# Two chained MLPs on one core: where the block-product weights of the second are built

## The chip, the cores and the metric

One NeuronCore of a Trainium2 chip runs the whole program. The metric is the device time of one execution in microseconds (us), as the median of several. Five engines work side by side, each through its own queue in order: PE (matmuls), ACT, DVE and POOL (elementwise work), and SP, which here issues all DMAs. Products are in float32, kept exact enough by splitting each operand into a rounded high half and a low half (operand minus high half) and adding three matmuls.

## The reference

Attention with packed keys gives x of 4608 tokens by 512. Two MLPs follow:

```python
a = x @ w_a;  b = x @ w_b                 # 512 -> 1536
y = (a * b) @ w_out                       # 1536 -> 512
h = y @ w_in                              # 512 -> 2048
g = h * clip(h + 3, 0, 6) / 6
out = g @ w_out2                          # 2048 -> 512
```

## The kernel before

The first MLP runs in four groups of 1152 tokens, each in twelve steps (`t`, with `m` = 0 to 11 inside a group) over the hidden width. In a step PE runs four `ab_unit` and one `pw_unit`; `y_unit`s follow three steps later and fill in between. Beside that, a list `bg` of small background units (Python functions that each emit a few instructions) is spread over the steps: in each step `nb` of them, `nb` being what is left of the list divided by the steps left before the last one, rounded up, and these over the step's ten slots. In the first three groups `bg` holds attention; in the last group (`g + 1 == NG`, 628 to 787 us in the profile) it holds the preparation of the second MLP: the y operands of the first tile of tokens (`y_units`) and the weights of the first block (`w_prep`). The last `y_unit`s run alone up to 806 us.

The second MLP runs over six tiles of 768 tokens (`tt`), each in eight blocks (`p`) of 256 hidden columns. A block computes its 2 x 2 block product h by the Strassen-Winograd scheme: seven products (`prod`, 6 matmuls of 384 columns each) in the order 1, 6, 2, 7, 5, 4, 3, into three PSUM banks' worth of results x, y and z that share two banks. DVE adds partial results (u2, u3, c22, c21, c12, all at L744), ACT and DVE apply the gate (`gate`, L751 and L753), and `parts` splits the gated block into g2h and g2l (L759, L760). Twelve output units (`o_unit`, three matmuls of 512 columns each) of the block before stand between the products: two after product 1, two after product 2, two after product 5, six after product 3. The first block of the first tile has none. In the profile the results are named h_px, h_py, h_pz for block p.

A product needs a weight operand out of `w` (128 x 3584 numbers per block: seven block matrices, high and low). Three of the seven are the raw blocks a11, a12, a22, four are sums of raw blocks. `w_prep` builds them once, in the first tile: `load` (L496) fetches two raw pieces, `wo_load` (L526) two raw pieces of the output weights, `sums` (L504 to L508) makes s1 to s4 on POOL, `parts` (L517, L518) copies to the high half on ACT and subtracts on POOL, `store` (L522) writes w to DRAM (`w2d`), and `wo_parts` (L533, L534) splits the output weights. The build of block p + 1 is put into the list `side` during block p. From the second tile on, `w_load` (L487) fetches the finished w, one block ahead. w has one buffer in each of two pools, used in turn. The raw weights, the raw output weights and the raw y data of the next tile (`y_load`, L546) all use one buffer, tag `raw`, in the pool `p2a`.

`side` is emptied in program order at fixed places of a block: `some(3)` after product 1 and two output units, `some(2)` after product 2, `some(2)` after product 5, `some(2)` and `some(9)` at the end. In block 6 of a tile the y load of the next tile and its three first differences on POOL (`y_first`) join the list. In block 7 `swap(k)` makes the next tile's operand for product k right after product k has run: a copy on ACT (L566) and a subtraction on DVE or POOL (L567).

Of the kernel before, what the change touches and what calls it, by code (L numbers as in the profile page):

```python
# [8 lines left out]
F32 = mybir.dt.float32  # L9
F32R = mybir.dt.float32r  # L10
# [11 lines left out]
DM, F1, F2 = 512, 1536, 2048  # L22
P = 128
# [7 lines left out]
NW = NM2 // 2  # L31
QK_SCALE = 1.0 / 8.0
CP = 512
# [7 lines left out]
def f32(ap):  # L41
    return ap.bitcast(F32)
# [3 lines left out]
def tile_kernel(ctx: ExitStack, tc: tile.TileContext, qT, kT, vn, pT, wab, wo1, win, wo2, out):  # L46
# [9 lines left out]
    act, dve, pool, pe, sp = nc.scalar, nc.vector, nc.gpsimd, nc.tensor, nc.sync  # L56
# [46 lines left out]
    p2f = dram.tile([NM2, 2, P, CP], F32, name="p2f")  # L103
# [378 lines left out]
    def w_tile(pool_, p, tt):  # L482
        w_t[p] = pool_.tile([P, 2, 7, 2, P], F32R, tag="w", name=f"w{tt}_{p}")
        return w_t[p]

    def w_load(pool_, p, tt):
        sp.dma_start(f32(w_tile(pool_, p, tt).rearrange("p h a k n -> p (h a k n)")), w2d[p])  # L487

    def w_prep(rpool, pool_, p):

        z = {}

        def load():
            z["r"] = rpool.tile([P, 6, CP], F32, tag="raw", name=f"raw_w{p}")
            for i in range(2):
                sp.dma_start(z["r"][:, i], p2f[2 * p + i, 0])  # L496

        def sums(lo):
            def fn():
                x = z["r"].rearrange("p i (k n) -> p i k n", k=2)  # L500
                a11, a12, a21, a22 = x[:, 0, 0], x[:, 0, 1], x[:, 1, 0], x[:, 1, 1]
                s1, s2, s3, s4 = x[:, 2, 0], x[:, 2, 1], x[:, 3, 0], x[:, 3, 1]
                if lo:
                    pool.tensor_sub(s3, a11, a21)  # L504
                    pool.tensor_sub(s4, a12, s2)
                else:
                    pool.tensor_add(s1, a21, a22)
                    pool.tensor_sub(s2, s1, a11)  # L508
            return fn

        def parts(of, a, n):
            def fn():
                if "w" not in z:
                    z["w"] = w_tile(pool_, p, 0).rearrange("p h a k n -> p h (a k n)")
                x = z["r"].rearrange("p i n -> p (i n)")[:, of * 256:(of + n) * 256]
                hi, lo = (z["w"][:, i, a * 256:(a + n) * 256] for i in range(2))
                act.copy(hi, x)  # L517
                pool.tensor_sub(lo, x, f32(hi))  # L518
            return fn

        def store():
            sp.dma_start(w2d[p], f32(z["w"].rearrange("p h x -> p (h x)")))  # L522

        def wo_load():
            for i in range(2):
                sp.dma_start(z["r"][:, 4 + i], p2f[2 * p + i, 1])  # L526

        def wo_parts(opool, i):
            def fn():
                hi = opool.tile([P, DM], F32R, tag=f"wo2_hi{p}{i}", name=f"wo2_hi{2 * p + i}")  # L530
                lo = opool.tile([P, DM], F32R, tag=f"wo2_lo{p}{i}", name=f"wo2_lo{2 * p + i}")
                wo2_t[2 * p + i] = (hi, lo)
                act.copy(hi, z["r"][:, 4 + i])  # L533
                pool.tensor_sub(lo, z["r"][:, 4 + i], f32(hi))  # L534
            return fn

        return [load, wo_load, sums(0), sums(1), parts(0, 0, 2), parts(3, 2, 1), parts(4, 3, 4), store], lambda o: [wo_parts(o, 0), wo_parts(o, 1)]

    def y_units(pool_, tt):

# [106 lines left out]
    p2a = None  # L647
# [16 lines left out]
    for t in range(NSTEP):  # L664
        g, m = divmod(t, NM1)
        if m == 0 and g + 1 < NG:
            lhs_tiles(g + 1)
            bg = att_units(2 * g + 2) + att_units(2 * g + 3)
        if m == 0 and g + 1 == NG:
            sp.dma_start(*stores[-1])  # L670
            es_att.close()
            p2a = es_p2a.enter_context(tc.tile_pool(name="p2a", bufs=1, side="right", reuse_waits="tile"))
            y_load, y_first, y_part = y_units(p2a, 0)
            prep, wo_prep = w_prep(p2a, p2a, 0)
            bg = [y_load, lambda: None, lambda: None] + y_first + [y_part[k] for k in (1, 6, 2, 7, 5, 4, 3)] + prep
# [12 lines left out]
        if t == 0:  # L688
            n_conv = 4
        elif g == 0:  # L690
            n_conv = sum(x < NM1 for x in (m + 2, m + 1, m + 3))
        else:
            n_conv = 2 * NM2 * (t - NM1 + 1) // (2 * NM1) - 2 * NM2 * (t - NM1) // (2 * NM1) if g < 3 else 0
        parts = spread(list(range(5 * n_conv)), 9 if n_conv > 2 else 6) + [[]] * 4
        now = []
        for i, (u, *x) in enumerate(units):
            if (u.__name__[:2], *x) not in ahead:
                u(*x)
            tick()
            if i == 1:  # L700
                wab_load(t + 3)
            if m % SW < 2 and i in ((3, 4) if t == 0 else (1, 2)):
                wo_split(t, i - (3 if t == 0 else 1))
            if m % SW == 1 and i in (3, 4):
                wo_split(t + 1, i - 3)
            if i in (3, 4) and m == NM1 - 1 and g + 1 < NG:
                at_split(2 * g + 3, (i - 3,))
            for k in range(2):
                for _ in parts[2 * i + k]:
                    if not now:  # L710
                        now = piece_units()
# [13 lines left out]
    with (  # L725
# [29 lines left out]
        def parts(i, j):  # L755
            n = 1 if i == j else 2
            hi, lo = tmp(f"g2h{i}{j}", n, F32R), tmp(f"g2l{i}{j}", n, F32R)
            u = u_t.pop((i, j))
            act.copy(hi, u)  # L759
            dve.tensor_sub(lo, u, f32(hi))  # L760
            g_t2[i, j] = (hi, lo)
# [32 lines left out]
                if side:  # L794
                    side.pop(0)()

        side.extend(wo_prep(p2b))
        for tt in range(NTT):
            for p in range(NW):
                now[:] = [tt, p]  # L800
                more = tt + 1 < NTT
                nxt = (p + 1) % NW
                wpool = (p2a, p2b)[nxt % 2]
                if tt == 0 and p + 1 < NW:
                    prep, wo_prep = w_prep(p2a, wpool, p + 1)
# [106 lines left out]
```

## Time and profile before

| | us |
|---|---|
| median of 3 runs (1589.46 to 1590.21) | 1590.19 |
| the profiled execution's own time | 1588.73 |
| its span, first to last instruction | 1587.0 |
| PE busy in the span | 1499.7 (95%) |
| DVE, ACT, POOL busy | 874.9, 682.0, 528.8 |

The rows below come from several views. The table of stretches gives, for each stretch, the busy time of each engine in it (x the number of its instructions), the granted clock of PE as a share of full speed, the busy share of the DMA engines and what they moved. A timeline lists instructions in order of time: start, duration, engine, line, operation, output <- inputs, and in brackets how long the engine sat idle before it and what ended that. A group row gives busy time and mean duration of equal instructions. A wait row says who waited for whom, the total, how often and the longest. A row of DMA issues gives the number, the size of each and the median time from issue to landing.

### The profile page before, as it was taken

Reading aid. Unit: us, or ns where it says so; the run is one execution under the profiler, and the core shown is the slowest. Engines: PE = TensorE matmul, PEld = TensorE weight load, DVE = VectorE, ACT = ScalarE, POOL = GpSimd, SP = SyncE. Lnnn points to the kernel's source line nnn. Section 1 sums busy time; section 2 is a strip of 40 time slices with the busy share of each in tenths; the row PEclk is TensorE's granted clock in tenths of the full one; section 3 lists DMA queues with packets and bytes.
Section 4 is the critical chain, followed back from the end, with each engine's and each line's share of the span. In section 5 each row is a group of like instructions: output and inputs, shape, how many; then the busy total and the mean of one; then the engine's idle time right before and its main releaser. Section 6 shows DMA issues by size and latency. Waiting matters only on the chain.

```text
span 1587.0 us, 27985 instructions
## 1 busy us (share of the span) xinstructions
PE 1499.7 (95%) x11128; PEld 1353.8 (85%) x11128; DVE 874.9 (55%) x1559; ACT 682.0 (43%) x1445; POOL 528.8 (33%) x508
## 2 busy tenths in 40 slices
PE   5598999989999899999989979999999999999998
PEld 2387999888989799999977868998998998998997
DVE  5778875555754666333346654455446455446443
ACT  4466644545455444453324433333334234324332
POOL 2566554353543445444436650020011011012000
PEclk8799999999999999999999989999999999999999
DMA  8665454644465333312143553334243343433431
GB/s 282 210 216 176 157 205 158 194 154 161 137 202 181 138 127 93 128 61 74 67 147 146 193 193 144 139 133 179 93 179 141 131 159 141 147 138 118 155 139 40
DMA packets 74946, 237.21 MB, mean 149 GB/s; under 512 B 7744, under 2 KB 26176, under 8 KB 68672
## 3 DMA queue, kind: packets, MB, share of 16 engines
q1 hardware_dynamic: 74816, 235.44, 42.9%
q8 instruction: 87, 1.43, 0.4%
q14 instruction: 43, 0.35, 0.1%
HBM read 184.03 MB, written 51.38 MB: 148 GB/s over the span
## 4 chain that ended last, share of the span: by engine, by line
PE 77%; DVE 5%; POOL 5%; issue 4%; ACT 4%; DMA 4%; SPq 1%; DVEq 0%; POOLq 0%; ACTq 0%
PE o L60 7%; PE o L61 7%; PE o L59 7%; PE y L59 6%; PE y L60 6%; PE y L61 6%; PE ab L59 6%; PE ab L61 6%; PE ab L60 6%; PE pw L412 2%; POOL w L518 2%; DMA raw_w<-p2f 2%; POOL wo_lo L534 1%; PE s L176 1%; DMA out<-os 1%
## 5 line engine op out<-in xcount | busy, mean ns | idle before, releaser
L59 PE MATMUL ab<-at_hi,pw_hi 128*128 128x288 f32 x768 | 233.5, 304 | 20.7 <-ACT a L438 17.2
L61 PE MATMUL ab<-at_hi,pw_lo 128*128 128x288 f32 x768 | 229.3, 299 | 4.5 <-DVE pw_lo L418 4.5
L59 PE MATMUL y<-g_hi,wo_hi 128*128 128x288 f32 x768 | 232.8, 303 | 0.4 <-DVE acc L467 0.4
L60 PE MATMUL ab<-at_lo,pw_hi 128*128 128x288 f32 x768 | 228.8, 298 | 1.8 <-POOL at_lo L292 1.8
L60 PE MATMUL y<-g_lo,wo_hi 128*128 128x288 f32 x768 | 228.1, 297 | 0.0
L61 PE MATMUL y<-g_hi,wo_lo 128*128 128x288 f32 x768 | 227.3, 296 | 0.0
L60 PE MATMUL o<-wo_lo,g2h 128*128 128x512 f32 x576 | 225.7, 392 | 0.0
L61 PE MATMUL o<-wo_hi,g2l 128*128 128x512 f32 x576 | 225.6, 392 | 0.0
L59 PE MATMUL o<-wo_hi,g2h 128*128 128x512 f32 x576 | 225.4, 391 | 0.0
L447 POOL TENSOR_TENSOR g_lo<-g,g_hi 128x288 fp32r<-128x288 f32 x192 | 162.3, 848 | 175.9 <-ACT g_hi L446 169.0
L760 DVE TENSOR_TENSOR g2l<-u,g2h 128x384 fp32r<-128x384 f32 x192 | 129.9, 677 | 149.0 <-ACT g2h L759 143.9
L440 DVE TENSOR_TENSOR g<-a,ab 128x288 f32<-128x288 f32 x192 | 86.8, 452 | 203.7 <-PE ab L61 132.9
L59 PEld LDWEIGHTS ab<-at_hi,pw_hi 128*128 128x128 f32 x768 | 146.5, 191 | 32.7 <-ACT a L438 19.3
L59 PEld LDWEIGHTS y<-g_hi,wo_hi 128*128 128x128 f32 x768 | 145.7, 190 | 18.9 <-issue 7.0
L558 POOL TENSOR_TENSOR ty_T<-raw_y 128x768 f32<-128x768 f32 x12 | 23.3, 1945 | 385.6 <-DMA raw_y<-y1d 385.6
L61 PEld LDWEIGHTS ab<-at_hi,pw_lo 128*128 128x128 f32 x768 | 146.6, 191 | 5.1 <-DVE pw_lo L418 5.1
L60 PEld LDWEIGHTS ab<-at_lo,pw_hi 128*128 128x128 f32 x768 | 146.5, 191 | 2.3 <-POOL at_lo L292 2.3
L751 ACT ACTIVATE r<-c,half_b 128x384 f32<-128x384 f32 x144 | 88.9, 617 | 136.7 <-DVE c L744 136.2
L60 PEld LDWEIGHTS y<-g_lo,wo_hi 128*128 128x128 f32 x768 | 145.7, 190 | 0.0
L61 PEld LDWEIGHTS y<-g_hi,wo_lo 128*128 128x128 f32 x768 | 145.6, 190 | 0.0
L759 ACT CAST g2h<-u 128x384 fp32r<-128x384 f32 x192 | 98.7, 514 | 98.3 <-DVE u L753 96.9
L438 ACT COPY a<-ab 128x288 f32<-128x288 f32 x192 | 76.2, 401 | 148.6 <-PE ab L61 147.0
(322 smaller groups left out, 3095.5 us busy)
## 6 DMA issues: line engine op xcount, KB each, us to landing
w<-w2d SPq DMA_DIRECT2D x40, 1792.0 KB, 7.3
rab<-wabf SPq DMA_DIRECT2D x36, 512.0 KB, 4.3
f64p<-in_wo SPq DMA_DIRECT2D x28, 512.0 KB, 3.7
w2d<-w SPq DMA_DIRECT2D x8, 1792.0 KB, 5.7
f64p<-in_wab SPq DMA_DIRECT2D x24, 512.0 KB, 4.1
k<-in_kT SPq DMA_DIRECT2D x16, 576.0 KB, 5.4
q<-in_qT SPq DMA_DIRECT2D x16, 576.0 KB, 5.5
ro<-wo1f SPq DMA_DIRECT2D x36, 256.0 KB, 2.9
```

The lines of the kernel that those rows point to most:

```text
L59: pe.matmul(ps, lhsT=l_hi, rhs=r_hi, start=first, stop=False, skip_group_check=skip)
L60: pe.matmul(ps, lhsT=l_hi, rhs=r_lo, start=False, stop=False, skip_group_check=skip)
L61: pe.matmul(ps, lhsT=l_lo, rhs=r_hi, start=False, stop=last, skip_group_check=skip)
L412: pe.matmul(ps[c][o, b, :], lhsT=l[r, b, q, :], rhs=w[r, q, :], start=True, stop=True)
L438: act.copy(a, ps[0])
L440: dve.tensor_mul(g32, a, ps[1])
L447: pool.tensor_sub(gl, g32, f32(gh))
L518: pool.tensor_sub(lo, x, f32(hi))
L558: pool.tensor_sub(z[to], get(a), get(b))
L751: act.activation(r, c, AF.Relu, bias=half_b, scale=1.0 / 6.0)
L759: act.copy(hi, u)
L760: dve.tensor_sub(lo, u, f32(hi))
```

## The change

All eight blocks' w are built in the last group of the first MLP, block 1 first and block 0 last, and stored; block 0's stays in its buffer. In the first tile `w_load` fetches w for the next block as in later tiles, as the first unit of the block's list; what remains there of the preparation is the output weights (`wo_prep`). The raw buffer holds two builds' pieces in turn, so the load of the next build is issued ahead of the sums of the present one. The low-half subtraction into w moves from POOL to DVE. The y operands of the first tile come behind the weight builds in the background list.

```diff
-    def w_prep(rpool, pool_, p):
+    def w_prep(pool_, ps):
...
-        def load():
-            z["r"] = rpool.tile([P, 6, CP], F32, tag="raw", name=f"raw_w{p}")
-            for i in range(2):
-                sp.dma_start(z["r"][:, i], p2f[2 * p + i, 0])
+        def load(i):
+            def fn():
+                if i == 0:
+                    z["r"] = pool_.tile([P, 6, CP], F32, tag="raw", name="raw_w")
+                for j in range(2):
+                    sp.dma_start(z["r"][:, 4 * (i % 2) + j], p2f[2 * ps[i] + j, 0])
+            return fn
...
-        def parts(of, a, n):
+        def parts(i, of, a, n):
             def fn():
-                if "w" not in z:
-                    z["w"] = w_tile(pool_, p, 0).rearrange("p h a k n -> p h (a k n)")
...
+                if a == 0:
+                    z["w"] = w_tile(pool_, ps[i], 0).rearrange("p h a k n -> p h (a k n)")
...
                 act.copy(hi, x)
-                pool.tensor_sub(lo, x, f32(hi))
+                dve.tensor_sub(lo, x, f32(hi))
             return fn
...
-        return [load, wo_load, sums(0), sums(1), parts(0, 0, 2), parts(3, 2, 1), parts(4, 3, 4), store], lambda o: [wo_parts(o, 0), wo_parts(o, 1)]
+        units = [load(0)]
+        for i in range(len(ps)):
+            units += [load(i + 1)] if i + 1 < len(ps) else []
+            units += [sums(i, 0), sums(i, 1), parts(i, 0, 0, 2), parts(i, 3, 2, 1), parts(i, 4, 3, 2), parts(i, 6, 5, 2), store(i)]
+        return units
+
+    def wo_prep(rpool, p):
...
+        def load():
+            z["r"] = rpool.tile([P, 2, CP], F32, tag="raw", name=f"raw_wo{p}")
             for i in range(2):
+                sp.dma_start(z["r"][:, i], p2f[2 * p + i, 1])
...
+            act.copy(hi, z["r"][:, i])
+            pool.tensor_sub(lo, z["r"][:, i], f32(hi))
...
-            prep, wo_prep = w_prep(p2a, p2a, 0)
-            bg = [y_load, lambda: None, lambda: None] + y_first + [y_part[k] for k in (1, 6, 2, 7, 5, 4, 3)] + prep
+            wo_load0, wo_parts0 = wo_prep(p2a, 0)
+            bg = w_prep(p2a, list(range(1, NW)) + [0])
+            bg += [y_load, lambda: None, lambda: None] + y_first + [y_part[k] for k in (1, 6, 2, 7, 5, 4, 3)] + [wo_load0]
...
-        side.extend(wo_prep(p2b))
+        side.extend([lambda i=i: wo_parts0(p2b, i) for i in range(2)])
...
+                if p + 1 < NW or more:
+                    side.insert(0, lambda x=(wpool, nxt, tt + (p + 1) // NW): w_load(*x))
                 if tt == 0 and p + 1 < NW:
-                    prep, wo_prep = w_prep(p2a, wpool, p + 1)
-                    side.extend(prep + wo_prep(p2b))
-                elif p + 1 < NW or more:
-                    side.append(lambda x=(wpool, nxt, tt + (p + 1) // NW): w_load(*x))
+                    load, parts2 = wo_prep(p2a, p + 1)
+                    side.extend([load, lambda: None, lambda: None] + [lambda f=parts2, i=i: f(p2b, i) for i in range(2)])
```

## Rows read from the trace of the kernel before

**Rows 1.** Table of stretches: last group, first tile, second tile (columns in the first line)
```profile
core 0: us, PE busy (x) PEld busy (x) DVE busy (x) ACT busy (x) POOL busy (x), PEclk, DMA share, GB/s
...
628.00:787.00 159.00, 158.98 (x1433) 151.73 (x1425) 57.30 (x117) 67.89 (x164) 74.79 (x85) 1.00 0.26 88
...
806.00:953.00 147.00, 126.41 (x601) 109.46 (x600) 87.01 (x108) 63.47 (x117) 89.67 (x72) 0.95 0.47 175
953.00:1078.00 125.00, 124.79 (x628) 112.75 (x627) 64.21 (x111) 45.66 (x83) 13.05 (x8) 1.00 0.39 144
```

**Rows 2.** Timeline of PE: starts in blocks 0, 1, 7, then 4 and 5 of tile two
```profile
807.23 0.33 PE L59 MATMUL h_0y<-yh_T,w 128*128 128x384 f32 x1
...
822.99 0.34 PE L59 MATMUL h_1y<-yh_T,w 128*128 128x384 f32 x1
...
924.67 0.34 PE L59 MATMUL h_7y<-yh_T,w 128*128 128x384 f32 x1
...
1015.40 0.39 PE L59 MATMUL o<-wo_hi,g2h 128*128 128x512 f32 x1
...
1016.08 0.33 PE L59 MATMUL h_4y<-yh_T,w 128*128 128x384 f32 x1
...
1031.59 0.34 PE L59 MATMUL h_5y<-yh_T,w 128*128 128x384 f32 x1
```

**Rows 3.** Instructions on tile h_0y, 950 to 958 us: durations, first and last start
```profile
L59 PE MATMUL h_0y<-yh_T,w x4: 333/334/334, 953.6 to 957.6; 128*128 128x384 f32 x4
```

**Rows 4.** Waits of PE, 780 to 960 us: total, times, longest
```profile
PE h_1x L61 <- POOL w L518: 4.4, 1, 4.4
```

**Rows 5.** Timelines of SP, POOL and PE in the first tile's last block
```profile
928.27 1.74 SPq L546 DMA_DIRECT2D raw_y<-y1d  x4
...
935.30 1.80 POOL L558 TENSOR_TENSOR ty_T<-raw_y,ty_T 128x768 f32<-128x768 f32 x1 [0.79 <-DMA raw_y<-y1d]
...
940.20 0.69 PE L59 MATMUL h_7z<-yh_T,w 128*128 128x384 f32 x1 [9.71 <-DVE u L753]
```

**Rows 6.** Groups by line and shape, DVE: 806 to 930 us, then 1080 to 1160
```profile
L760 DVE TENSOR_TENSOR g2l<-u,g2h 128x384 fp32r<-128x384 f32 x28 | 27.1, 969 | 31.6 <-ACT g2h L759 30.7
...
L760 DVE TENSOR_TENSOR g2l<-u,g2h 128x384 fp32r<-128x384 f32 x20 | 11.1, 556 | 15.8 <-ACT g2h L759 15.2
```

**Rows 7.** DMA issues: whole span, then 854 to 866 us, then 1038 to 1060
```profile
w<-w2d SPq DMA_DIRECT2D x40, 1792.0 KB, 7.3
...
w2d<-w SPq DMA_DIRECT2D x8, 1792.0 KB, 5.7
...
raw_w<-p2f SPq DMA_DIRECT2D x32, 256.0 KB, 4.0
...
w2d<-w SPq DMA_DIRECT2D x1, 1792.0 KB, 7.9
...
raw_y<-y1d SPq DMA_DIRECT2D x4, 384.0 KB, 8.3
```

**Rows 8.** Timeline of ACT in block 5 of the second tile: its first two gates
```profile
1033.93 0.58 ACT L751 ACTIVATE r<-h_5x,half_b 128x384 f32<-128x384 f32 x1 [2.63 <-PE h_5x L61]
...
1037.97 0.62 ACT L751 ACTIVATE r<-c,half_b 128x384 f32<-128x384 f32 x1 [2.27 <-DVE c L744]
```

**Rows 9.** Timelines of SP and POOL around the start of the first tile
```profile
787.28 19.91 SPq L469 DMA_DIRECT2D y1d<-acc  x16
...
808.51 2.56 POOL L534 TENSOR_TENSOR wo_lo<-raw_w,wo_hi 128x512 fp32r<-128x512 f32 x2 [17.01 <-ACT wo_hi L533]
```

**Rows 10.** Groups by line and shape in the last group and its end, 628 to 806
```profile
L418 DVE TENSOR_TENSOR pw_lo<-pw,pw_hi 128x512 fp32r<-128x512 f32 x22 | 14.1, 683 | 4.1 <-ACT pw_hi L414 4.0
...
L517 ACT CAST w<-raw_w 128x512 fp32r<-128x512 f32 x1 | 0.6, 619 | 0.0
```

**Rows 11.** Waits: ACT's, 628 to 806 us, then PE's in the group before, 450 to 628
```profile
ACT a L438 <- PE ab L61: 43.4, 36, 2.3
...
PE ab L59 <- ACT a L438: 4.5, 2, 4.1
```

More of the change, by code (lines that the diff above doesn't have):

```diff
@@ L487, in w_load, with blocks, sums @@
         sp.dma_start(f32(w_tile(pool_, p, tt).rearrange("p h a k n -> p (h a k n)")), w2d[p])
-    def w_prep(rpool, pool_, p):
+    def w_prep(pool_, ps):
         z = {}
-        def load():
-            z["r"] = rpool.tile([P, 6, CP], F32, tag="raw", name=f"raw_w{p}")
-            for i in range(2):
-                sp.dma_start(z["r"][:, i], p2f[2 * p + i, 0])
-        def sums(lo):
-            def fn():
-                x = z["r"].rearrange("p i (k n) -> p i k n", k=2)
-                a11, a12, a21, a22 = x[:, 0, 0], x[:, 0, 1], x[:, 1, 0], x[:, 1, 1]
-                s1, s2, s3, s4 = x[:, 2, 0], x[:, 2, 1], x[:, 3, 0], x[:, 3, 1]
+        def load(i):
+            def fn():
+                if i == 0:
[3 more added lines that the diff above has]
+            return fn
+        def blocks(i):
+            x = z["r"].rearrange("p i (k n) -> p i k n", k=2)
+            return [x[:, 4 * (i % 2) + j, k] for j in range(2) for k in range(2)] + [x[:, 2 + j, k] for j in range(2) for k in range(2)]
+        def sums(i, lo):
+            def fn():
+                a11, a12, a21, a22, s1, s2, s3, s4 = blocks(i)
                 if lo:
@@ L509, in sums @@
             return fn
-        def parts(of, a, n):
+        def parts(i, of, a, n):
             def fn():
-                if "w" not in z:
-                    z["w"] = w_tile(pool_, p, 0).rearrange("p h a k n -> p h (a k n)")
-                x = z["r"].rearrange("p i n -> p (i n)")[:, of * 256:(of + n) * 256]
-                hi, lo = (z["w"][:, i, a * 256:(a + n) * 256] for i in range(2))
+                if a == 0:
+                    z["w"] = w_tile(pool_, ps[i], 0).rearrange("p h a k n -> p h (a k n)")
+                of_ = of + 8 * (i % 2) if of < 4 else of
+                x = z["r"].rearrange("p i n -> p (i n)")[:, of_ * 256:(of_ + n) * 256]
+                hi, lo = (z["w"][:, j, a * 256:(a + n) * 256] for j in range(2))
@@ L517, in fn @@
                 act.copy(hi, x)
-                pool.tensor_sub(lo, x, f32(hi))
+                dve.tensor_sub(lo, x, f32(hi))
             return fn
-        def store():
-            sp.dma_start(w2d[p], f32(z["w"].rearrange("p h x -> p (h x)")))
-        def wo_load():
-            for i in range(2):
[L526 to L535, printed above, removed]
@@ L537, in w_prep, with store @@
-        return [load, wo_load, sums(0), sums(1), parts(0, 0, 2), parts(3, 2, 1), parts(4, 3, 4), store], lambda o: [wo_parts(o, 0), wo_parts(o, 1)]
+        def store(i):
+            return lambda: sp.dma_start(w2d[ps[i]], f32(z["w"].rearrange("p h x -> p (h x)")))
+        units = [load(0)]
+        for i in range(len(ps)):
+            units += [load(i + 1)] if i + 1 < len(ps) else []
+            units += [sums(i, 0), sums(i, 1), parts(i, 0, 0, 2), parts(i, 3, 2, 1), parts(i, 4, 3, 2), parts(i, 6, 5, 2), store(i)]
@@ new lines, in w_prep, with parts @@
+        return units
+    def wo_prep(rpool, p):
+        z = {}
+        def load():
+            z["r"] = rpool.tile([P, 2, CP], F32, tag="raw", name=f"raw_wo{p}")
+            for i in range(2):
+                sp.dma_start(z["r"][:, i], p2f[2 * p + i, 1])
+        def parts(opool, i):
+            hi = opool.tile([P, DM], F32R, tag=f"wo2_hi{p}{i}", name=f"wo2_hi{2 * p + i}")
+            lo = opool.tile([P, DM], F32R, tag=f"wo2_lo{p}{i}", name=f"wo2_lo{2 * p + i}")
+            wo2_t[2 * p + i] = (hi, lo)
+            act.copy(hi, z["r"][:, i])
+            pool.tensor_sub(lo, z["r"][:, i], f32(hi))
+        return load, parts
```

## The prediction

> **What bounds the kernel now.** I read the table of stretches first, then PE's own waits, then the timeline around the two waits that matter. In the table [rows 1] the reader is to look at PE's busy time against the length of each stretch: in the last group of the first MLP (628 to 787 us) PE has 158.98 of 159 us, in the second tile of the second MLP (953 to 1078) 124.79 of 125, but in the first tile (806 to 953) only 126.41 of 147, and there the granted clock is 0.95 where it is 1.00 before and after. So PE is the bound everywhere around the change, and the first tile is the one place where it is short of work. How much it loses there comes from the starts of the second product (h_ky) of each block [rows 2] and of the next tile [rows 3]. A steady block lasts 1031.59 - 1016.08 = 15.5 us, and an output unit 0.68 us (1015.40 to 1016.08), so twelve of them are 8.2 us and the 42 product matmuls 7.3 us, or 1.04 for each of the seven products. The first block has no output units. Without a wait the first tile would run from 807.23 for 7.3 us plus the two output units ahead of the next block's second product (1.4), which puts h_1y at 815.9, and then seven blocks of 15.5 us to the next tile: 117.2 us. It takes 953.6 - 807.23 = 146.4. **The loss is 29.2 us**: 7.1 us before h_1y (it starts at 822.99), 8.7 us in the six blocks up to h_7y (924.67 - 822.99 = 101.7 against 93.0), and 13.4 us in the last block (953.6 - 924.67 = 28.9 against 15.5). Their causes: PE waits 4.4 us for POOL's low half of the second block's weights [rows 4], and 9.7 us in the last block because the next tile's y data came late [rows 5]. The rest is DVE next to POOL: its low-half subtraction L760 takes 969 ns in this tile and 556 ns in the next [rows 6].
>
> **What leaves the first tile.** Per block go one raw load, four POOL sums, the POOL subtractions into w, the ACT copies into w and a store; seven times. In their place stands w_load, one transfer of 1792 KB, median 7.3 us to landing [rows 7], and the small load of the output weights. From the third block on I cost both at nothing. w_load is issued when the buffer's last reader, the seventh product of the block before, is done. Behind that product still run six output units (4.1 us), and the block that reads the data comes a whole block later, so 7.3 us lie within 19 us; later tiles do just this without a wait (124.79 of 125 us). The copy of the output weights is an ACT instruction behind the first gate, whose r ends 5.3 us into a block (1033.93 + 0.58, the block starting 2.4 us before its h_ky, at 1029.2) [rows 8]. Its load, if first in line, takes 4.0 us, and 8.3 us is what the y loads need when a w load is ahead [rows 7]. Counted from 4.1 us before the block it lands between 0.1 us before the block's start and 4.2 us into it, before ACT asks for it in either case. If that cover were gone, what is late next is DVE's c22 and with it PE's seventh product, which begins 9.6 us into a block; only a landing later than some 7 us would cost PE anything.
>
> **What remains of the loss.** (a) Block 0. SP's queue holds the sixteen y1d stores in front of w_load, and the last of them goes out at 787.28 + 19.91 = 807.2 [rows 9]; 7.3 us later is 814.5, near PE's own end of the block (814.5). The raw load for block 1's output weights can go out only when POOL has finished the two subtractions of block 0's (808.51 + 2.56 = 811.1) [rows 9], and it has the w load ahead of it: it lands between 815.1 (4.0 us) and 819.4 (8.3 us). I take 816, nearer the first, as most of the w load has passed by 811. ACT stands at that copy from about 813.5; behind it in ACT's queue are the copies and gates from which DVE makes c12 (0.6 for the copy and four steps of 0.5 to 0.6), and c12 frees the PSUM bank of block 1's second product. So h_1y starts at about 819 instead of 815.9: 3 us, bounds 2 and 6.5. (b) Block 1 has the same chain half a block later, its raw load issued only near 821: 0.7 us, bounds 0 and 3. (c) The last block. The y load needs the raw buffer, which is free after the second output-weight copy: behind the second gate's r (ends 9.4 us into block 6 [rows 8]), plus ACT 0.6 [rows 10] plus POOL 1.3, so at 11.3 us. From that issue to PE's fifth product the trace of before needs 940.20 - 928.27 = 11.9 us [rows 5], so the product can start 23.2 us after block 6 began, 7.7 us into block 7. PE gets there by itself at four products and four output units, 6.9 us. Wait 0.8 us instead of 9.7, bounds 0 and 4. Together 4.5 us remain, between 2 and 13.5.
>
> **What the first MLP's last group takes on.** Seven more weight builds: 16 small loads, 28 POOL sums, 28 ACT copies, 28 low-half subtractions (now on DVE), and eight stores instead of one. The list of background units grows from 21 to 78, so 8 go into the first step and 7 into each of ten more; a step is 159/12 = 13.3 us, a unit about 1.9 us. Sums of time: ACT 8 x (3 x 0.62 + 0.4) = 18 us, less the 2 of the one build there now; DVE 8 x (3 x 0.68 + 0.4) = 20 us (619 ns for the copy, 683 ns for a subtraction of that width) [rows 10]. ACT would be busy 84 of 159 us and DVE 77; POOL's 75 us lose one build's subtractions and gain 28 sums, at most 36 us even at the 1.28 us that an output-weight subtraction of twice the width takes [rows 9]: none is a bound by its sum. What counts is queue order. **The added wait** is at the first copy of each build into w, since w has one buffer here: it must wait for the store of the build before. From the last copy to the next first copy are five units, 9.5 us; in between stand the copy 0.6, the DVE subtraction 0.7 (up to 2.5 if it runs into a POOL instruction), SP's issue 0.3 and the store's 5.7 us (7.9 the longest) [rows 7]: 7.3 to 11.4 us. So ACT is held by 0 to 1.9 us, seven times. Behind it in ACT's queue are the copies a out of PSUM, and PE waits for those; ACT sits idle for PE 43.4/36 = 1.2 us ahead of them [rows 11], which covers most of it. The y preparation moves to the last two of the eleven steps, one load of 1.5 MB and three POOL differences in a row; the y products of those steps need only low halves made before, so I cost it at nothing; if that cover is gone POOL is some 3 us late once. The nearest row for all this is the group before, in which attention units fill the same slots: there PE lost 4.5 us to ACT's a, in 2 waits [rows 11]. I take 2 us, bounds 0 and 12 (seven times 1.9 minus nothing covered). A gain is excluded here: PE is already at 158.98 of 159.
>
> **A rule against it.** What the rows show of DVE next to POOL is L760's 969 ns against 556 [rows 6]. The Trainium skill (SBUF — State Buffer, Who interferes with whom) says that a DVE instruction with two SBUF inputs and a GpSimd instruction that reads SBUF exclude each other for the whole instruction; the moved subtractions are of that kind. By that rule 32 of them would now stand between POOL's subtractions in the saturated group.
>
> **Sum.** 29.2 - 4.5 - 2 = 22.7 us less. The profiled execution took 1588.73 us (span 1587.0), 1.46 us under the median of the runs shown; 1588.73 - 22.7 = 1566.0, or **1567.5 us** as a median.
>
> **The rivals.** *Contention in the last group*: each of the 32 DVE subtractions meets a POOL instruction, g_lo (0.8 us) or a difference, and PE's accumulators and g products wait behind it. For it: 0.4 us more per subtraction is what rows 6 give, 13 us in all. Against it: half of DVE's time there is waiting for PE. If all of it came through instead of the 2 us: 1578. *The last block's wait stays*, because the output-weight copy of block 7 is late behind the w load, or POOL's three differences are: 12.6 of the 13.4 us come back, 1580. For it: the y data are still behind the same raw buffer. Against: the buffer is freed in the middle of block 6, not at the start of block 7. *Slower: the store of w holds ACT.* One mechanism, at the first copy of each of seven builds: if the store lands late, because it stands in SP's queue behind loads that wait for buffers, ACT and then PE stand still. It decides from 24.7/7 = 3.5 us of PE per build, so from a store landing later than 12.6 us (9.5 - 1.6 + 1.2 + 3.5). At 16 us, twice the longest in the trace, 7 x 6.9 = 48 us go and the time is 1588.73 + 1.46 + 48 - 24.7 = 1614. Against it: stores of 5.7 us at the median and 7.9 at the longest [rows 7]. *It does not do what it says*: w_load takes over as the late operand in every block; a landing of 7.3 us against 19 speaks against it; 1590.
>
> **How the numbers follow.** Forecast 0.70; contention 0.12; last block 0.10; slower 0.06; no effect 0.02. The forecast's own bounds are 1563 (2 us remain, nothing lost in the group) and 1576. The range 1560 to 1580 takes in the first three, and leaves out some of the tails. 0.2% is 3 us, about what a measurement of this kernel can tell from no change: faster 0.92, same 0.02, slower 0.06.
>
> **What would show it.** In the profile after: no POOL sums beyond some 780 us; h_1y about 12 us after h_0y; blocks 2 to 6 at 15.5 us; a wait of PE near 1 us before h_7z; the first tile about 122 us long and its clock at 1.00; the last group 0 to 4 us longer, with ACT's waits at the copy into w under 2 us. The prediction is wrong if that group grows by more than 6 us, if w_load lands after its block began, or if PE still waits 5 us and more before h_7z.

## The result and the profile after

The changed kernel takes **1569.07 us** (median of four runs, 1567.94 to 1570.58) against 1589.83 us for the kernel before (four runs, 1587.14 to 1590.21). The ratio is 0.9875, its 95% interval 0.9862 to 0.9889. The profiled execution has a span of 1566.7 us, 20.3 us less than before.

Table of stretches, kernel after: the last group, the first tile, the second tile (length, busy us of each engine with its instructions, granted clock, DMA share, GB/s).

```profile
core 0: us, PE busy (x) PEld busy (x) DVE busy (x) ACT busy (x) POOL busy (x), PEclk, DMA share, GB/s
628.00:787.00 159.00, 156.68 (x1404) 148.79 (x1404) 79.62 (x147) 79.31 (x190) 90.41 (x107) 1.00 0.53 188
808.00:930.00 122.00, 117.70 (x595) 105.70 (x594) 63.35 (x105) 49.75 (x92) 32.87 (x22) 1.00 0.48 173
930.00:1054.00 124.00, 123.12 (x621) 111.36 (x620) 63.77 (x111) 44.88 (x82) 13.20 (x7) 1.00 0.38 141
```

Against [rows 1], PE loses 20.6 of 147 us in the first tile before and 4.3 of 122 after, the clock there is 1.00 instead of 0.95, and POOL has 33 us of work in it instead of 90. The bill stands in the first line: PE, which had no gap in the last group, now has 2.3 us of it, and POOL and DVE carry 16 and 22 us more.

Timeline of PE after: start, duration, instruction, and in brackets how long PE stood idle and for what.

```profile
783.55 0.40 PE L59 MATMUL ab<-at_hi,pw_hi 128*128 128x288 f32 x1 [1.69 <-ACT a L438]
784.88 0.40 PE L59 MATMUL ab<-at_hi,pw_hi 128*128 128x288 f32 x1 [0.28 <-ACT a L438]
...
810.00 0.33 PE L59 MATMUL h_0y<-yh_T,w 128*128 128x384 f32 x1
...
817.42 0.41 PE L59 MATMUL h_1x<-yh_B,w 128*128 128x384 f32 x1 [0.52 <-DMA w<-w2d]
...
821.38 0.45 PE L59 MATMUL h_1y<-yh_T,w 128*128 128x384 f32 x1 [1.31 <-DVE c L760]
...
837.54 0.33 PE L59 MATMUL h_2y<-yh_T,w 128*128 128x384 f32 x1
...
915.03 0.34 PE L59 MATMUL h_7y<-yh_T,w 128*128 128x384 f32 x1
...
920.76 0.44 PE L59 MATMUL h_7z<-yh_T,w 128*128 128x384 f32 x1 [1.08 <-DVE u L769]
...
925.40 0.45 PE L59 MATMUL h_7z<-yh_B,w 128*128 128x384 f32 x1 [0.91 <-DVE c L760]
...
933.06 0.33 PE L59 MATMUL h_0y<-yh_T,w 128*128 128x384 f32 x1
```

Two lengths carry what follows. **The tile** runs from h_0y to the next tile's h_0y: 933.06 - 810.00 = 123.06 us, where [rows 2, 3] gave 146.4. **The group** runs from its first pw matmul (626.70 us here, 627.03 before) to h_0y: 183.30 us, before 180.20. So the tile gives 23.3 us and the group takes 3.1: 20.2 us, which is the 20.3 of the spans. The group's start lies between 626.7 and 630 us in the traces read here, whatever is edited behind it, so a total blurs an edit that is worth 1 or 2 us. Each experiment is therefore read from the stretch that it touches. Each length comes from one profiled execution. Intervals and blocks 1 to 6 that no edit touches repeat to a few hundredths, but block 0 and block 7 spread more (11.16 to 11.59 and 17.69 to 18.51 us in kernels whose edit isn't aimed at them), so a few tenths there say nothing. The ratio is to runs of the kernel before made beside each kernel.

| kernel | median us | ratio to before (95%) | group | tile | block 0 | block 7 |
|---|---|---|---|---|---|---|
| before | 1589.8 | | 180.20 | 146.37 | 15.76 | 28.93 |
| after | 1569.07 | 0.9875 (0.9862 to 0.9889) | 183.30 | 123.06 | 11.38 | 18.03 |
| e1, y first | 1570.27 | 0.9878 (0.9863 to 0.9892) | 184.02 | 123.49 | 11.33 | 18.51 |
| e2, store in two | 1569.28 | 0.9868 (0.9850 to 0.9886) | 183.99 | 122.54 | 11.16 | 17.73 |
| e3, own buffer | 1567.36 | 0.9856 (0.9841 to 0.9871) | 183.35 | 120.91 | 11.43 | 15.83 |
| e4, e1 to e3 together | 1567.6 | 0.9859 (0.9843 to 0.9875) | 183.40 | 120.79 | 11.28 | 15.87 |
| e5, stored twice | 1591.08 | 1.0012 (1.0003 to 1.0022) | 205.05 | 123.29 | 11.59 | 18.06 |
| e6, before with DVE | 1583.36 | 0.9961 (0.9946 to 0.9976) | 180.21 | 140.61 | 12.34 | 28.03 |
| e7, w load last | 1576.36 | 0.9917 (0.9896 to 0.9938) | | | | |
| e8, low half on POOL | 1569.98 | 0.9878 (0.9862 to 0.9895) | 185.81 | 123.42 | 11.50 | 18.27 |
| e9, T4 on DVE | 1567.23 | 0.9862 (0.9846 to 0.9879) | 180.86 | 123.33 | 11.48 | 18.20 |
| e10, four edits | 1567.21 | 0.9862 (0.9847 to 0.9876) | 179.99 | 123.07 | 14.24 | 15.85 |
| e11, e7 again | 1576.36 | 0.9918 (0.9903 to 0.9933) | 183.32 | 129.26 | 18.59 | 17.69 |
| e12, three edits | 1562.65 | 0.9835 (0.9822 to 0.9849) | 179.97 | 120.62 | 11.11 | 15.87 |

e7's profiled execution ran at a mean granted clock of 0.74 (1867.29 us) and is left out: its median is that of the other three, and the lengths of this kernel are e11's. A block's length is from its h_ky to that of the next. Blocks 2 to 6 last 15.49 to 15.51 us after the change, as in a later tile; before they took 16.4 to 17.1.

In the group, ACT's timeline shows two places where it stood; SP's shows the store ahead of the first.

```profile
746.49 0.93 ACT L523 CAST w<-raw_w 128x512 fp32r<-128x512 f32 x2 [3.71 <-issue]
...
782.37 0.83 ACT L581 CAST yh_T<-ty_T 128x768 fp32r<-128x768 f32 x1 [3.06 <-POOL ty_T L573]
```

```profile
739.78 0.32 SPq L528 DMA_DIRECT2D w2d<-w  x1
```

```profile
w2d<-w SPq DMA_DIRECT2D x8, 1792.0 KB, 6.7
```

The first is the wait that the change added: the store of the build before goes out at 739.78 and needs 6.7 us by the last row (the median of the eight), so it lands near 746.5, when the copy starts. The releaser is written as "issue", yet the times name the store. PE feels it in one interval between two pw products, the ninth, which lasts 13.22 us instead of 12.37. The second lies at the group's end: the y operand yh_T waits for the last of POOL's four differences (T4 in the code), the copies a stand behind it in ACT's queue, and PE waits 1.69 and 0.28 us for them. From the last pw product to h_0y it is 40.97 us instead of 38.46. (The seventh interval was 0.25 us longer before; that closes the 3.1.)

### The profile page after: what moved, and what is told of

The parts are those of the page before. It is cut to its first block, busy times and chain, and to the rows that moved or that the text cites. A ratio compares the mean times of both kernels' runs of the same rounds, so it can differ in the third digit from the quotient of the medians.

```text
span 1566.7 us, 28001 instructions
## 1 busy us (share of the span) xinstructions
PE 1494.0 (95%) x11128; PEld 1351.5 (86%) x11128; DVE 876.7 (56%) x1591; ACT 683.2 (44%) x1453; POOL 490.9 (31%) x484
## 4 chain that ended last, share of the span: by engine, by line
PE 82%; DVE 6%; ACT 4%; DMA 4%; issue 2%; POOL 1%; SPq 1%; DVEq 0%; ACTq 0%; POOLq 0%
PE o L60 8%; PE o L61 8%; PE o L59 8%; PE y L59 7%; PE y L60 6%; PE y L61 6%; PE ab L59 5%; PE ab L61 5%; PE ab L60 5%; PE pw L412 2%; PE s L176 1%; DVE cv_ap L88 1%; DMA out<-os 1%; DMA k<-in_kT 1%; DVE cv_ap L84 1%
## 5 line engine op out<-in xcount | busy, mean ns | idle before, releaser
L447 POOL TENSOR_TENSOR g_lo<-g,g_hi 128x288 fp32r<-128x288 f32 x192 | 163.8, 856 | 164.8 <-ACT g_hi L446 159.3
L776 DVE TENSOR_TENSOR g2l<-u,g2h 128x384 fp32r<-128x384 f32 x192 | 121.9, 635 | 141.1 <-ACT g2h L775 136.1
```

What stands on the lines that cost most here:

```text
L447: pool.tensor_sub(gl, g32, f32(gh))
```

## The experiments

**e1: does the late y preparation cost the group's end?** The y units go to the front of the list.

```diff
-bg = w_prep(p2a, list(range(1, NW)) + [0])
-bg += [y_load, ...] + y_first + [y_part[k] for k in (1, 6, 2, 7, 5, 4, 3)] + [wo_load0]
+bg = [y_load, ...] + y_first + [y_part[k] for k in (1, 6, 2, 7, 5, 4, 3)]
+bg += w_prep(p2a, list(range(1, NW)) + [0]) + [wo_load0]
```

> The changed kernel with one edit: in the background list of the last group the first tile's y operands stand ahead of the weight builds again, as before the change. Theory: of the 3.1 us that the group grew, some 2 us are the y preparation at its end (the copy of T4 waits 3.1 us for POOL's difference, and PE 1.7 + 0.3 us behind it), and they go: h_0y at about 808 instead of 810, total 2 us less, near 1567. Rival: the group grew by the builds themselves (the store that ACT waits for, DVE beside POOL), which the order does not touch: no change, 1569, and the 2 us wait turns up behind another copy.

The end of the group is free again (38.46 us), but the second and third interval are 15.15 and 14.85 us instead of 13.56 and 12.36, and the group is no shorter (184.02). The waits of the group, e1 (who for whom, total, times, longest):

```profile
PE y L60 <- POOL g_lo L447: 2.2, 1, 2.2
...
ACT yh_T L581 <- POOL ty_T L573: 2.9, 1, 2.9
```

So the late place is not the cause, and the 2 us that were expected back did not come: the y units hold seven POOL instructions of 1.84 us each (four differences, three low halves), and they make POOL late at either place, because the list gives them to it within two steps.

**e2: is the hold of ACT the store?** The store goes in two parts: the first three of the seven matrices leave right behind the copies that finish them, the other four at the end. All builds then use one w tile, so that the first copy of the next build waits for the first part alone.

```diff
-units += [..., parts(i, 3, 2, 1), ..., parts(i, 6, 5, 2), store(i)]
+units += [..., both(parts(i, 3, 2, 1), store(i, 0, 3)), ..., parts(i, 6, 5, 2), store(i, 3, 4)]
```

> The changed kernel with one edit: all builds use one w tile, and its store goes out in two parts, the first (matrices 1 to 3) after the second copy, the rest at the end, so that the first copy of the next build waits only for the first part, which left two units earlier. Theory: ACT's two waits for the store (3.7 and 1.2 us) go and with them 0.9 us of PE: total 0.9 us less, about 1568. Rival: the hold is covered anyway (PE waits somewhere else for the same time): no change.

ACT no longer waits at the copy into w, and the ninth interval is 12.37 us, as before the change, so the hold was the store. The group is no shorter all the same: the 0.85 us come back, and 0.7 more, behind the last pw product (42.51 us). The waits there are the same 1.69 and 0.28 us as in the changed kernel; what differs is the clock behind them. PE's stretches of 2 us, first after, then e2:

```profile
785.00:787.00 2.00, 2.00 (x16) 1.00 0.03 8
787.00:789.00 2.00, 2.00 (x18) 1.00 0.69 200
789.00:791.00 2.00, 2.00 (x18) 1.00 0.21 80
```

```profile
785.00:787.00 2.00, 1.72 (x10) 0.72 0.03 8
787.00:789.00 2.00, 2.00 (x10) 0.50 0.46 96
789.00:791.00 2.00, 2.00 (x16) 0.93 0.43 166
```

In e2 the granted clock goes to 0.50, the 1.2 GHz level, after these waits, and PE does 36 matmuls in 6 us instead of 52. The waits cost 2 us; whether a lower clock follows, and with it some 1.5 us more, differed between kernels that hardly differ there: behind the same two waits it stays at 1.00 in e3 and e11 as well, and goes to 0.50 in e8 too.

**e3: does the raw buffer set the last block?** The output weights get raw buffers of their own, so that the y load need not wait for the second copy.

```diff
-z["r"] = rpool.tile([P, 2, CP], F32, tag="raw", name=f"raw_wo{p}")
+z["r"] = rpool.tile([P, 2, CP], F32, tag="raw" if p == 0 else "rawo", name=f"raw_wo{p}", bufs=1 if p == 0 else 2)
...
-load, parts2 = wo_prep(p2a, p + 1)
+load, parts2 = wo_prep(p2b, p + 1)
```

> The changed kernel with one edit: the raw output weights of blocks 1 to 7 get two buffers of their own, so that neither they nor the next tile's y load wait for the shared raw buffer. Theory: the y load goes out at the start of block 6 as in later tiles, PE's two waits in block 7 (1.1 and 0.9 us) go, and block 7 lasts 15.5 to 16 us instead of 18.1; at the start of the tile the output weights of block 1 are issued 3 us earlier but land behind the w load, so at most 1 us comes back there: total 2 to 3.5 us less, 1566. Rival: block 7 is late because of POOL's differences and not because of the buffer: no change.

The y load, SP's timeline in the changed kernel and then in e3, which also shows block 0's two loads:

```profile
813.86 0.80 SPq L543 DMA_DIRECT2D raw_wo<-p2f  x2
...
908.44 1.74 SPq L561 DMA_DIRECT2D raw_y<-y1d  x4
```

```profile
812.41 0.38 SPq L487 DMA_DIRECT2D w<-w2d  x1
812.89 0.88 SPq L543 DMA_DIRECT2D raw_wo<-p2f  x2
...
896.94 2.32 SPq L561 DMA_DIRECT2D raw_y<-y1d  x4
```

Counted from h_0y the y load leaves 13.9 us sooner, and block 7 drops from 18.03 to 15.83 us: the buffer was nearly the whole of that wait. Block 0 stays at 11.43, though its small load now goes out right behind the w load instead of 3.3 us later. It lands at the same point, and ACT waits for it as long as in the changed kernel. ACT's timelines, after and e3:

```profile
817.98 0.62 ACT L549 CAST wo_hi<-raw_wo 128x512 fp32r<-128x512 f32 x1 [1.92 <-DMA raw_wo<-p2f]
```

```profile
820.40 0.62 ACT L549 CAST wo_hi<-raw_wo 128x512 fp32r<-128x512 f32 x1 [1.98 <-DMA raw_wo<-p2f]
```

From h_0y to this copy it is 8.0 us in both. It lands 0.7 us after the w load in both, so the 1792 KB ahead of it set its landing, not the buffer.

**e4: e1, e2 and e3 together.**

> The changed kernel with the three edits together: y operands first, store in two parts, own buffers for the output weights. Theory: the three causes lie on PE's path one after the other, so they add: 5 to 6.5 us less than the changed kernel, about 1563.5. Rival: what one edit frees is lost at the next late operand (the builds now end last in the group): 1566 to 1567.

Group 183.40, tile 120.79: e3's gain stands, e1 and e2 add nothing to it. The second and third interval are 15.19 and 14.19 us, the end 38.47. So the rival holds: moving the y units only moves POOL's backlog, and with them in front ACT has no long hold at the store any more (e1's ninth interval is 12.37 us too), which leaves the split nothing to free.

**e5: what would a late store cost?** Each build is stored twice, first into a second array in DRAM.

```diff
-sp.dma_start(w2d[ps[i]], f32(z["w"]...))
+for d in (w2x, w2d):
+    sp.dma_start(d[ps[i]], f32(z["w"]...))
```

> The changed kernel with each store of w doubled, to a second array in DRAM first and then to its own (14.7 MB more are written). It puts a price on the rival that forecast a slower kernel: ACT held at the first copy of each build by the store before. Theory: the two stores land about 5 us later than the one, 11 to 12 us after the issue; ACT is then held 3 to 5 us seven times and PE loses what its 1.2 to 2 us of cover leave, 2 to 3 us each: 14 to 20 us more, 1583 to 1589, which is near the kernel before. Rival: the hold is absorbed by the y_units and pw_units that stand between: under 5 us more, below 1574.

```profile
w2d<-w SPq DMA_DIRECT2D x8, 1792.0 KB, 11.1
```

```profile
PE ab L59 <- ACT a L439: 13.0, 5, 5.1
...
PE y L59 <- ACT acc L466: 3.2, 2, 2.6
...
ACT w L524 <- DMA w2d<-w: 24.6, 5, 8.3
ACT w L524 <- issue: 4.6, 2, 2.7
```

The second store lands after 11.1 us instead of 6.7. ACT stands at the first copy of each of the seven later builds, 29.2 us in all (the two holds put down to "issue" end when the store lands, like the five others). The group grows by 21.75 us, a little more than the 14 to 20 expected; nothing else moves, and the time is that of the kernel before (1.0012). Not all of the 21.75 us are waits. PE stands 16.6 us in the group, 14.3 more than in the changed kernel. Behind three of its waits the granted clock is at 0.50; two of these stretches (length, PE busy, clock, DMA share, GB/s):

```profile
710.00:717.00 7.00, 4.68 (x19) 0.51 0.27 110
765.00:771.50 6.50, 5.69 (x24) 0.50 0.29 118
```

With the third (805.8 to 809.2 us) PE works 13.8 us at half clock, which by this count costs it some 7 us and makes up most of the rest. So the waiting copy is the place where this change could have lost everything: 4.4 us more per store are enough.

**e6: how much is only POOL?** In the kernel *before*, the low half of w goes from POOL to DVE, nothing else.

```diff
-pool.tensor_sub(lo, x, f32(hi))
+dve.tensor_sub(lo, x, f32(hi))
```

> The kernel before with one part of the change alone: the low-half subtraction into w is done by DVE instead of POOL; everything else, the place of the builds too, as before. Theory: the 29 us of the first tile come from the chain load, sums, copy, use that runs once per block there, and POOL's subtractions are some 5 of the 12 us of that chain: 5 to 12 us come back, 1578 to 1585. Rival: it is the sharing of POOL and DVE alone (L760 at 969 ns against 556) that makes the first tile slow: 20 us and more come back, 1569 or less.

The tile loses 5.8 us (146.37 to 140.61), a quarter of what the change takes off it. DVE's groups in the first tile, kernel before and then e6, whose second line answers to [rows 6]:

```profile
L753 DVE SCALAR_TENSOR_TENSOR u<-r,c 128x384 f32<-128x384 f32 x21 | 26.6, 1265 | 5.6 <-ACT r L751 5.2
```

```profile
L753 DVE SCALAR_TENSOR_TENSOR u<-r,c 128x384 f32<-128x384 f32 x21 | 12.1, 578 | 7.7 <-ACT r L751 7.3
L760 DVE TENSOR_TENSOR g2l<-u,g2h 128x384 fp32r<-128x384 f32 x28 | 23.9, 853 | 9.1 <-ACT g2h L759 8.2
...
PE h_7z L59 <- DVE u L753: 9.7, 1, 9.7
```

With the subtractions into w off POOL, DVE's gate takes 578 ns instead of 1265, although DVE has more to do; but the last block's wait is 9.7 us as it was. So most of the gain is not the engine but the place: the builds, and what they hold up, are out of the tile. e8 below shows it from the other side: with the builds moved and the low half still on POOL, the tile is 123.42 us.

**e7 and e11: must the w load be the first of its block?** It goes behind the small load. Both are the same kernel; the trace is e11's.

```diff
-side.insert(0, lambda x=...: w_load(*x))
...
+side.insert(1 if tt == 0 and 0 < p < NW - 1 else 3 if tt == 0 and p == 0 else 0, lambda x=...: w_load(*x))
```

> The changed kernel with one edit: in the first tile w_load stands behind the load of the raw output weights in the list of a block, and so in SP's queue, instead of ahead of it. Theory: in block 0 that small load waits for the raw buffer until POOL is done (813.9 in the changed kernel), so w_load leaves near 815 instead of 810 and lands near 822 instead of 817: block 1 starts 4 to 5 us later, the other blocks are as before: 1573 to 1574. Rival: block 1 waits for its output weights and not for w; they land earlier when they are first in line: 0 to 1 us less, 1568 to 1569.

> The kernel with w_load behind the raw output weights in the list of the first tile, again, for a trace at full clock. Theory: w_load of block 1 leaves at about 815 us and lands at about 822, so block 0 (h_0y to h_1y) lasts 15 to 17 us instead of 11.4 and the other blocks are unchanged, total 1573 to 1575. Rival: other blocks lose too, because the raw buffer of every block is freed late and w_load now waits for it: 0.5 us and more in each of blocks 1 to 6.

```profile
815.62 0.80 SPq L543 DMA_DIRECT2D raw_wo<-p2f  x2
816.51 0.38 SPq L487 DMA_DIRECT2D w<-w2d  x1
...
PE h_1x L59 <- DMA w<-w2d: 7.2, 1, 7.2
```

In block 0 the load stands in SP's queue behind one that waits for a buffer. It goes out 4.7 us after h_0y instead of at once, PE waits 7.2 us for it, and block 0 lasts 18.59 us instead of 11.38. Both expectations were too low (15 to 17 us for the block, at most 1575 for the whole, where 1576.36 was measured): the load takes 9.2 us here instead of 7.2, and the clock, for which neither had a term, is at 0.50 behind the wait, from 823.4 to 830.2 us. Blocks 2 to 6 do not change (15.49 us): there the load has slack, in the first block it has none.

**e8: do DVE and POOL get into each other's way in the group?** The low half goes back to POOL, in the changed kernel.

```diff
-dve.tensor_sub(lo, x, f32(hi))
+pool.tensor_sub(lo, x, f32(hi))
```

> The changed kernel with one edit: the low-half subtraction into w stays on POOL, as before the change, at the new place in the last group. Theory: POOL takes 1.3 us where DVE takes 0.83, so each store leaves 1 to 3 us later, ACT is held longer at the next build, and POOL (90 of 159 us busy, then 123) makes its g low halves late: 2 to 8 us more, 1571 to 1577. Rival (contention): 32 DVE instructions that meet POOL's reads are what made the group longer; without them 1 to 3 us less, 1566 to 1568.

Table of stretches, e8, and then two groups of DVE in the changed kernel: a subtraction that was there before, and the moved ones.

```profile
628.00:787.00 159.00, 155.77 (x1423) 147.55 (x1422) 56.90 (x113) 78.09 (x187) 122.48 (x139) 1.00 0.54 190
```

```profile
L418 DVE TENSOR_TENSOR pw_lo<-pw,pw_hi 128x512 fp32r<-128x512 f32 x22 | 14.1, 679 | 0.0
L524 DVE TENSOR_TENSOR w<-raw_w,w 128x512 fp32r<-128x512 f32 x24 | 19.9, 831 | 14.8 <-ACT w L523 14.8
```

On DVE a subtraction takes 831 ns beside POOL, where I had taken 683 from [rows 10]. That row was of another kind: pw lies in PSUM, raw_w and w in SBUF. The 22 subtractions from PSUM take 674 to 684 ns each, whether POOL is at work or not; those into w take 677 to 1240 ns, and the two longest begin 0.69 us before an instruction of POOL (L447) ends. The Trainium skill (SBUF — State Buffer, Who interferes with whom) lets a DVE instruction with two SBUF inputs and a GpSimd instruction that reads SBUF exclude each other. The trace shows a delay of that sort, of 0.15 us on average, and no wait of PE that comes from it. On POOL the same work costs the group 2.5 us more (185.81). The ninth interval is 14.27 us, 1.05 more, and ACT stands at the copy into w 8.0 us in 3 waits. The end is 42.43 us, 1.5 more, but the waits of PE there are those of the changed kernel (1.70 and 0.28 us); what is added is the clock, at 0.50 from 787.4 to 790.9 us, as in e2. That this comes from POOL is not shown: the profiled execution took 1572.72 us, the three others 1569.22 to 1570.03, and the median is only 0.9 us above the changed kernel's. So DVE was the better place by about 1 us, less than the 2 to 8 expected.

**e9: is the end of the group POOL's backlog?** Only the fourth difference goes to DVE.

```diff
-pool.tensor_sub(z[to], get(a), get(b))
+(dve if to == "T4" and tt == 0 else pool).tensor_sub(z[to], get(a), get(b))
```

> The changed kernel with one edit: the difference T4 of the first tile's y operands is taken by DVE instead of POOL. The run with y first showed that the order does not decide; now the theory is that the 2.5 us at the group's end are POOL's backlog (it is busy without a break from 765 to 778 us in the changed kernel, and T4 with it), on which ACT's copy waits. Then DVE, idle for 4.5 us there, makes T4 some 3 us earlier: from the last pw of the group to h_0y 38.5 to 39.3 us instead of 40.97, total 2 us less, near 1567. Rival: the step simply carries too many units for ACT and DVE, whoever makes T4: no change, 40.5 to 41.5.

```profile
ACT yh_T L581 <- DVE ty_T L573: 0.4, 1, 0.4
...
PE ab L59 <- ACT a L438: 0.2, 1, 0.2
```

ACT waits 0.4 us for T4 instead of 3.1, the end is 38.51 us, 2.5 less, and the group 180.86. One instruction on another engine is the whole of it; the ninth interval still has the store's 0.87.

**e10: e2, e3 and e9 together, and block 0's small load ahead of the w load.**

```diff
+if p == 0:
+    side.insert(0, load)
```

> The changed kernel with four edits: store in two parts, T4 on DVE, own buffers for the output weights of blocks 1 to 7, and in block 0 their load ahead of w_load in SP's queue (it needs no POOL work now). Theory: the group falls from 183.3 to 180.3 to 181 us (first pw to h_0y), block 0 from 11.4 to 10.5, block 7 from 18.0 to 15.8: 5 to 6 us less than the changed kernel, 1563 to 1564. Rival: a part that is freed is lost at the next late operand, as with the three edits before: 1566 to 1567.

The group is 179.99 and block 7 15.85 us: both gains add up. Block 0, though, is 14.24. ACT waits for the small load no longer; now the w load is late:

```profile
820.23 0.66 PE L59 MATMUL h_1x<-yh_B,w 128*128 128x384 f32 x1 [3.42 <-DVE u L777]
```

```profile
809.84 0.87 SPq L551 DMA_DIRECT2D raw_wo<-p2f  x2
810.81 6.35 SPq L487 DMA_DIRECT2D w<-w2d  x2
```

```profile
w<-w2d SPq DMA_DIRECT2D x1, 1792.0 KB, 9.3
```

The wait is put down to DVE, but the w load goes out at 810.81 and lands 9.3 us later, at 820.1, where PE goes on. Behind 512 KB it takes 9.3 us, in front 7.3. (Part of block 0's 14.24 us is again the clock, at 0.50 from 819.6 to 823.1 us behind the wait.) In either order one of the two is late, and the small one is the cheaper: block 0 then lasts 11.1 to 11.6 us.

**e12: e10 without that.**

> The kernel with four edits without the fourth: store in two parts, T4 on DVE and own buffers for the output weights, w_load first in block 0 again. Theory: w_load is the last operand of block 1, and the 0.5 MB ahead of it cost 2.9 us there; then block 0 lasts 11.2 to 11.5 us instead of 14.2, the group 180.0 and block 7 15.8 as in the run with four edits: 2.5 to 3 us less than that run and 5 to 6 less than the changed kernel, 1563.5 to 1565. Rival: block 0 was long for the larger number of buffers in the second pool, so that w_load's target came free later: 14 us again, 1567.

1562.65 us (1562.21 to 1563.48), ratio 0.9835 (0.9822 to 0.9849), the best of all: group 179.97 us, no longer than before the change, block 0 11.11 and block 7 15.87 us. In the table of stretches PE is busy again without a gap in the group:

```profile
628.00:787.00 159.00, 159.00 (x1430) 152.03 (x1428) 81.80 (x150) 80.87 (x193) 91.16 (x109) 1.00 0.56 192
```

In the group, then, POOL and DVE carry about the same sums as in the changed kernel, the moved subtractions stand on DVE beside POOL as there, and it costs nothing: the 3.1 us were two places in the queues.

## Why the prediction was right, point by point

The forecast was 22.7 us less for the profiled execution; it is 20.2. Sign, mechanism and size hold; two terms were too small, what remains in the tile by 1.4 us and the cost of the group by 1.1.

- *The loss of 29.2 us in the first tile* is the right frame: blocks 2 to 6 go to 15.5 us, the clock to 1.00, and only blocks 0, 1 and 7 keep something. 123.06 - 117.2 = 5.9 us remain, where the sum had 4.5. Its split was misread, though: what the two waits leave, 15.1 us, is not all DVE next to POOL. PE's idle time is 20.6 us of the loss. Some 4 us more are the clock: behind the two long waits PE worked at 0.50, from 819.5 to 822.3 us and, longer, in this stretch of the kernel before:

```profile
940.20:945.00 4.80, 4.80 (x13) 0.50 0.00 0
```

  e6 puts 5.8 us on the engine that subtracts. The sum does not hang on the split, since it counts only what remains; but some 4 of the 23.3 us gained are clock that came back with the waits.
- *Block 0: 3 us said, 2.7 measured* (11.38 instead of 8.7). The raw load lands 8.0 us after h_0y, where I took 8.8, and c12 is the operand that PE waits 1.31 us for, as said. What I had called near, the w load, is a limit of its own: PE waits 0.52 us for it. e3, e10 and e11 show that the two loads delay each other; none of the orders tried gets the block below 11.1 us.
- *Block 1: 0.7 said, 0.66 measured.*
- *Block 7: 0.8 said, 2.5 measured*, the term that was too small in the tile. Its first half holds nearly to the tenth: the y load leaves at 908.44, which is 11.3 us after block 6 began (2.4 us before its h_6y, at 899.5), as the sum had it, and PE waits 1.08 us before the fifth product. But I followed the chain to that product only. The seventh waits another 0.91 us: the bank that it writes is freed by DVE's c22, and ahead of that in DVE's queue stands the low half of the next y operand, late by the same chain and 2.60 us long. DVE's timeline after:

```profile
922.28 2.60 DVE L582 TENSOR_TENSOR yl_T<-ty_T,yh_T 128x768 fp32r<-128x768 f32 x1
924.80 0.54 DVE L760 TENSOR_TENSOR c<-u,h_7z 128x384 f32<-128x384 f32 x1
```

  With the y load early (e3) all of it but 0.3 us is gone.
- *The group: 2 us said, 3.1 measured.* **The step that was mis-sized is the y preparation, priced at nothing.** It costs 2.5 us. The text had its cover and price ("if that cover is gone POOL is some 3 us late once") and the cover was gone: POOL is busy without a pause from 762.5 to 778.2 us, its fourth difference ends at 782.3, and ACT stands 3.06 us. I had argued from the products that need the data; those were not late. The place where it hurts is ACT's queue, where the y copy stands ahead of the copies that PE needs next. e1 and e9 show it from two sides. That 2 came near 3.1 is partly luck: the 2 us were taken from the group before and meant above all for the holds at the store, which cost 0.86, and the term put at nothing cost more than all of them.
- *The added wait* was right in place and nearly in size: said were 0 to 1.9 us seven times, mostly covered. The trace has one hold of 3.7 us and one of 1.2, of which 0.86 us reach PE. e2 and e5 show that it is the store. (The upper bound of 12 us is given as seven times 1.9, which is 13.3; and the forecast's own end of 1576 us is not its upper bounds added up, which give 1586. Neither moves the forecast.)
- *The rivals.* Contention: DVE's subtractions are 0.15 us slower than priced, not 0.4, and PE waits for none of them. The last block's wait: 2.0 of 9.7 us is left. The slower one has the right place; e5 shows it. Its point of decision was put at a store of 12.6 us, and with 11.1 the gain is already gone. Its price of the waits was right: 11.1 + 1.6 - 9.5 - 1.2 = 2.0 us per build, 14 in all, and PE stands 14.3 us more in e5, in holds of ACT of 1.2 to 8.3 us, not seven equal ones. What it had no term for is the clock at 0.50 behind three of them, most of the other 7.5 us.
- *The signs.* h_1y comes 11.4 us after h_0y (about 12 said), the tile is 123.06 us (about 122), and blocks 2 to 6, the wait before h_7z and the clock are as said. Two signs missed: ACT's wait at the copy into w was to stay under 2 us and is 3.7 once; and the w load of block 1 lands 0.5 us after PE is ready for that block, which the text had named as a sign of being wrong. It costs that 0.5 us, and in no other block does PE wait for w.

Open is why the clock stays at 1.00 behind the group's last two waits in the changed kernel, e3 and e11 and goes to 0.50 in e2 and e8; one execution of each was profiled, so it may differ from execution to execution and not from kernel to kernel.

## What to carry to other kernels

Work that is moved from a short stage into a full one is paid for not by the engines' sums but where a moved instruction that waits stands ahead of one that the bounding engine needs: go through the moved work, for each of its waits name the next instruction in that queue, and price that. Here 3.1 us of cost were one store and one subtraction; with both out of the way, and one buffer split, the same move gives 1.65% instead of 1.25%. Price a long wait of the bounding engine above its length where the clock falls behind it: in e5 that was about a third of the loss. And where small edits are compared, measure the stretch that each touches: a start that wanders by 3 us hides them in the total.

## What the runs showed of the hardware that was not expected

- Two loads in the same queue delay each other, and order decides which: 1792 KB land in 7.3 us when first and 9.3 us behind 512 KB. The small load, sent 3.3 us sooner behind the large one, did not land sooner (e3).
- After the same two waits of 1.97 us in sum, PE's granted clock stayed at 1.00 in three kernels (after, e3, e11) and fell to 0.50 for 3.4 us in two (e2, e8), which cost 1.5 us more than the waits. It also fell with PE's waits of 4.4 and 9.7 us in the kernel before, of 3.4 us in e10 and of 7.2 us in e11.
- A DVE gate of 128x384 that takes 578 ns in e6 took 1265 ns in the kernel before, where POOL did the subtractions of w, a wider gap than the 969 against 556 ns of the low-half subtraction that the prediction had looked at.
- A DVE subtraction of 128x512 with one input in PSUM took 674 to 684 ns beside a busy POOL, one with both inputs in SBUF 677 to 1240 ns (e8's rows of the changed kernel).
